# Three products of a weight conversion change engines: two from GpSimd to VectorE, one from VectorE to GpSimd

## The chip, the cores and the metric

The kernel runs on one core of one Trainium2 chip. A core has a matrix engine (TensorE, PE in the profile, with its weight loads shown as PEld), a vector engine (VectorE, DVE), a scalar engine (ScalarE, ACT), a general engine (GpSimd, POOL) and SyncE (SP), which here only starts transfers. Each engine runs its own list of instructions in order and waits for others through semaphores. The metric is the device time of one execution in microseconds, less is better; a time is the median of the runs shown. Before the change it is 257.74 us, the median of 3 runs from 257.5 to 257.95.

## The reference

A linear attention with product features is followed by a two-layer perceptron with exact GELU:

```python
def phi(x):                                   # r = 8, so 64 features
    a = np.einsum('rd,bhsd->bhsr', S1, x)
    b = np.einsum('rd,bhsd->bhsr', S2, x)
    return np.einsum('bhsi,bhsj->bhsij', a, b).reshape(*x.shape[:-1], r * r)
q_p, k_p = (phi(q), phi(k))                   # q, k, v: (4, 4, 1088, 32) float32
kv = np.einsum('bhsf,bhsd->bhfd', k_p, v)
z = np.sum(k_p, axis=2)
num = np.einsum('bhsf,bhfd->bhsd', q_p, kv)
den = np.einsum('bhsf,bhf->bhs', q_p, z)[..., None] + 1e-06
x = (num / den).transpose(0, 2, 1, 3).reshape(4352, 128)
h = x @ w_in                                  # w_in: (128, 2048) float64
g = 0.5 * h * (1.0 + erf(h / sqrt(2)))
out = g @ w_out                               # w_out: (2048, 128) float64
```

The two weights and the sketches S1 and S2 arrive as float64. The kernel computes in float32: it takes the two 32-bit words of each number apart and makes a float32 of them.

## The kernel before, in words

**Tiling.** The 4352 tokens are worked on as chunks of 512: two chunks for each of the four batches, and a ninth chunk that holds the 64 tokens left over of each batch. Tokens of a chunk lie in the free dimension, `xT[n]` being 128 x 512. For each chunk `hidden(n, fi)` multiplies one 128-column tile of w_in with `xT[n]` (line 770) and ScalarE applies GELU (line 777). There are 16 such tiles, fi = 0 to 15. The second product takes one of two forms. The first four tiles of chunk 0 and the first eight of chunk 1 are projected plainly (`project`, line 955). All others go through a Strassen-like scheme of seven products instead of eight, in blocks of four tiles: `token_sums` (lines 821 to 824, on GpSimd) makes four sums of a block's GELU outputs, `channel_sums` (lines 808 to 811, on GpSimd) makes four sums of each piece of w_out into the tiles T1 to T4, once, and `two_products` (line 856) multiplies them on TensorE, two products at a time, one in either half of the array's columns.

**Weights.** Both weights come in five pieces of 256, 256, 512, 512 and 512 columns: `w_in[0..4]` and `w_out[0..4]`. In the text, piece 4 of w_in is the last one, for the tiles fi = 12 to 15, and piece 2 of w_out the third one, for fi = 4 to 7. The class `Rounding` converts a piece. `fields` (VectorE, lines 283 and 288) cuts exponent and mantissa bits out of the high words; `low_words` and `exponents` (ScalarE, lines 270 and 294) scale the low words and rebias the exponents; `mantissas` (VectorE, line 302) joins the mantissa's two parts; `signs` (VectorE, line 307) adds the sign to the exponent; `product` (line 312) multiplies mantissa and signed power of two into the float32 weight. `product` takes the engine as an argument, VectorE unless told otherwise; `finish` is mantissas, signs and product on VectorE.

**Order.** The order of every engine's list is the order of the text; nothing is planned at run time. After a start in which the first attention chunk is made, a loop walks over steps t, one `hidden` call each. Steps 0 to 3 are tiles 0 to 3 of chunk 0, steps 4 to 11 tiles 0 to 7 of chunk 1, steps 12 to 23 the other tiles of chunk 0, steps 24 to 31 the other tiles of chunk 1, then chunk after chunk. Steps 0 to 3 have their side work written out by hand: there the pieces 0 and 1 of w_out are converted, with their products on GpSimd, and `ratio` (lines 686 to 700) makes chunk 1's `xT` on VectorE. At step 4 the projections of chunk 0's tiles 0 to 3 (two of them issued at step 3 already) and the two halves of chunk 1's first hidden product (`first_hidden`, line 786) follow. Later steps have lists `slots[t]`, filled by `at(t, f, ...)` in the order in which the calls are written. The six pieces from index 2 on are converted in turns, w_in before w_out: the fields of a turn are cut before the turn in front of it is ended. `end` of w_in's last piece stands in step 12, that of w_out's last piece in step 13, behind the two transposes of the next keys (`key_turn_blocks`, line 383). The channel sums of pieces 1, 0, 2, 3 and 4 stand in steps 5, 6, 13, 16 and 18. `widen_v_rem(1)` (line 366, GpSimd) in step 12 waits for a transfer. The token sums of chunk 0's blocks are issued at steps 15, 19 and 23, and their products start four, three and three steps later.

**What later work reads.** The projections of chunk 0 read w_out's pieces 0 and 1. `hidden` of steps 20 to 23 reads w_in's last piece. The seven-product blocks read T1 to T4 and the token sums.

Of the kernel before, what the change touches and what calls it, by code (L numbers as in the profile page):

```python
# [16 lines left out]
def kernel(  # L17
# [18 lines left out]
    pe, dve, act, pool, sp = nc.tensor, nc.vector, nc.scalar, nc.gpsimd, nc.sync  # L36
# [31 lines left out]
    def work_banks():  # L68

        return wps.tile([128, 2, CW], FP, name="w_ps")  # L70
# [505 lines left out]
    def expand_copy(n, i):  # L576
        A[i] = att.tile([128, 2, CW // 2], FP, name="A_sb")
        act.copy(out=A[i][:, :, :width[n] // 2], in_=B_of[n, i][:, :, :width[n] // 2])

    def expand_multiply(n, i):  # L580
        W = width[n]
        a, b = (t.rearrange("f g (r x) -> f g r x", r=2) for t in (A[i][:, :, :W // 2], B_of[n, i][:, :, W // 2:W]))
        dve.tensor_mul(out=qp[n].rearrange("f r (g x) -> f g r x", g=G)[:, 2 * i:2 * i + 2], in0=a, in1=b)  # L583
# [90 lines left out]
    def ratio_products(n, banks):  # L674

        for s in range(2):
            for c in range(NP):
                rows = slice(c * F, (c + 1) * F)
                for r in range(2):
                    for i, (h, w) in enumerate(((2 * c + r, kz_apart[rows, r, c, :D]), (2 * (1 - c) + r, z_cols[rows, r]))):  # L680
                        pe.matmul(banks[h * D:(h + 1) * D, i, s * HW:(s + 1) * HW], lhsT=w,
                                  rhs=qp[n][rows, r, s * HW:(s + 1) * HW], start=True, stop=True)

    def ratio_turn(banks):
        turned = att.tile([128, 2 * CW], FP, name="q_f", bufs=1)
        dve.transpose(out=turned[:, :CW], in_=banks[:, 1])
        return turned

    def ratio(n, banks, turned):

        den = att.tile([128, NP, 2 * H], FP, name="den_tok").rearrange("p c k -> p (c k)")
        first = turned[:, :CW].rearrange("p (k x) -> p k x", x=D)[:, :, 0]
        for c in range(NP):
            dve.tensor_scalar(out=den[c * F:(c + 1) * F], in0=first[(1 - c) * F:(2 - c) * F], scalar1=1e-6, scalar2=None, op0=AX.add)
        dve.reciprocal(out=den, in_=den)
        xT[n] = att.tile([128, CW], FP, name="xT", bufs=3)
        for s in range(2):
            wide = turned[:, CW + s * HW:CW + (s + 1) * HW]
            dve.transpose(out=wide, in_=den[:, s * 8:(s + 1) * 8, None].broadcast_to([128, 8, D]))
            dve.tensor_mul(out=xT[n][:, s * HW:(s + 1) * HW], in0=banks[:, 0, s * HW:(s + 1) * HW], in1=wide)  # L700
# [63 lines left out]
    def hidden(n, fi, by_halves=False):  # L764
        W = width[n]
        ps = first_banks.pop((n, fi)) if (n, fi) in first_banks else hidden_bank()
        w = w_tile(w_in_sb, fi)
        for rows in (slice(0, 64), slice(64, 128)) if by_halves else (slice(0, 128),):
            if (n, fi) not in begun:
                pe.matmul(ps[rows, :W], lhsT=w[:, rows], rhs=xT[n][:, :W], start=True, stop=True)  # L770
        if n < NCH and fi < USUAL[n]:
            g_of[n, fi] = mlp.tile([128, CW], FP, name="g", bufs=4)
        else:
            if fi % NB == 0:
                blocks[n, fi // NB] = block(FP)
            g_of[n, fi] = blocks[n, fi // NB][:, fi % NB]
        act.activation(out=g_of[n, fi][:, :W], in_=ps[:, :W], func=ACT.Gelu)  # L777

    def first_hidden(n, half):

        if half == 0:
            first_banks[n, 0] = hidden_bank()
        parts = 1 if n else 2
        for i in range(parts):
            cols = slice(half * 256 + i * 256 // parts, half * 256 + (i + 1) * 256 // parts)
            pe.matmul(first_banks[n, 0][:, cols], lhsT=w_tile(w_in_sb, 0), rhs=xT[n][:, cols], start=True, stop=True)  # L786
# [53 lines left out]
    def first_block(n):  # L840
        return USUAL[n] // NB if n < NCH else 0
# [102 lines left out]
    def project(n, fi, parts=range(B // 2), cols=slice(None)):  # L944
        first, final = fi == (BLOCKED if n == NMAIN else 0), fi == (USUAL[n] if n < NCH else NF) - 1
        if first and n not in o_of:
            o_of[n] = out_bank() if n < NMAIN else [out_bank() for i in range(B // 2)]
        g = g_of[n, fi]
        if n == NMAIN:

            for i in parts:
                pe.matmul(o_of[n][i][:, :128], lhsT=g[:, i * 128:(i + 1) * 128], rhs=w_tile(w_out_sb, fi),  # L952
                          start=first, stop=final)
            return
        pe.matmul(o_of[n][:, cols], lhsT=w_tile(w_out_sb, fi), rhs=g[:, cols], start=first, stop=final)  # L955
# [35 lines left out]
    r = Rounding(SR)  # L991
# [43 lines left out]
    w_out = [Rounding(w, beside=b) for w, b in zip(w_out_sb[:2], w_in)]  # L1035
# [28 lines left out]
    def at(t, f, *a):  # L1064
        slots[t].append(lambda: f(*a))
# [88 lines left out]
    rounding = {}  # L1154

    def begin(w):

        rounding[w.name] = Rounding(w)
        rounding[w.name].fields()

    def by_scalar(w, *what):
        for f in what:
            getattr(rounding[w.name], f)()

    def end(w):
        rounding[w.name].finish()

    turns = [w[i] for i in range(2, 5) for w in (w_in_sb, w_out_sb)]
    both, low, exp = ("low_words", "exponents"), ("low_words",), ("exponents",)
    schedule = (((4, exp),), ((5, low), (6, exp)), ((7, both),), ((8, low), (9, exp)), ((10, both),), ((11, low), (12, exp)))  # L1170
    for k, acts in enumerate(schedule):
        t1 = acts[-1][0]
        if k + 1 < len(turns):
            at(t1, begin, turns[k + 1])
        for t, what in acts:
            at(t, by_scalar, turns[k], *what)
        if k + 1 < len(turns):
            at(t1, end, turns[k])
    at(12, widen_v_rem, 1)
    for i, t in ((1, 5), (0, 6), (2, 13)):  # L1180
        at(t, channel_sums, i)
    at(16, channel_sums, 3)
    for r in range(2):
        at(13, key_turn_blocks, 1, r)
    at(13, end, turns[-1])
    at(16, features_of_all, 1)
    at(16, outer_of_all, 1)
# [93 lines left out]
    for t in range(len(steps) + LAG):  # L1281
        if t < 4:

            hidden(0, t)
            if t == 0:
                expand_multiply(1, 0)
                w_out[0].fields()
                expand_copy(1, 1)
                expand_multiply(1, 1)
            if t == 1:  # L1290
                w_out[0].low_words()
                w_out[0].exponents()
                w_out[0].mantissas()
                w_out[0].signs()
                w_out[0].product(pool)
                w_out[1].fields()
            if t == 2:
                w_out[1].low_words()
            if t == 3:
                banks = work_banks()  # L1300
                ratio_products(1, banks)
                w_out[1].mantissas()
                w_out[1].exponents()
                turned = ratio_turn(banks)
                w_out[1].signs()
                w_out[1].product(pool)
                ratio(1, banks, turned)
                project(0, 0)
                project(0, 1)
            continue  # L1310
        if t == 4:
            begin(turns[0])
            by_scalar(turns[0], *low)
            for f, *a in products[t] + products[t + 1]:
                f(*a)
            for half in range(2):
                first_hidden(1, half)
        for n in drains[t]:
            drain(n)
        sooner = t == NMAIN * NF  # L1320
        if sooner:
            for f, *a in products[t]:
                f(*a)
        if t < len(steps):
            n, fi = steps[t]
            hidden(n, fi, by_halves=t >= 18)
        if t < len(steps) and steps[t][0] < NMAIN and steps[t][1] % NB == NB - 1:
            n, b = steps[t][0], steps[t][1] // NB
            if b >= first_block(n):
                token_sums(n, b)  # L1330
        for f in slots[t]:
            f()
        for n in done[t]:
            store(n)
        if t not in (4, 5) and not sooner:
            for f, *a in products[t]:
                f(*a)
# [41 lines left out]
```

## Time and profile before

| what | value |
|---|---|
| median of 3 runs | 257.74 us (257.5 to 257.95) |
| the profiled execution's own time | 257.98 us |
| its span in the profile | 256.1 us |
| PE busy | 252.0 us, 98% |
| DVE busy | 160.8 us, 63% |
| ACT busy | 113.4 us, 44% |
| POOL busy | 177.4 us, 69% |
| granted TensorE clock | 0.999 |

Starts in the profile are counted from the beginning of the span; 1.88 us of the execution's own time lie around it. A row of the timeline has the start, the duration, the engine, the line, the operation, the tile written and the tiles read, the shape and the count; what stands in brackets at its end is the idle time of the engine just before it and what ended that. A float32 matrix product appears as two weight loads and two matmuls, so a 512-column product of one tile is two rows. Instructions of one engine overlap a little: a VectorE row of 0.42 us is followed by the next after 0.34 us where nothing ties them, and a 128x512 GpSimd row of 1.28 us after 1.23 us.

### The profile page before, as it was taken

The page shows a single profiled execution, that of the slowest core. Times are in us where ns is not written, and L with a number is a line of the kernel's source. Part 1 is how long each engine was busy: PE and PEld are TensorE (multiplying, and loading weights), DVE is VectorE, ACT ScalarE, POOL GpSimd, SP SyncE. Part 2 cuts the span into 40 slices and gives each one's busy share as a digit, 9 for nine tenths or more (in the row PEclk, how much of TensorE's full clock was granted, in tenths as well). Part 3 has the DMA queues.
Part 4 walks back from the last instruction along what each step waited for, and adds up shares of the span by engine and source line. Part 5 has one row for each costly group of instructions (what it writes and reads, how often), then busy time and mean ns, then how long its engine had stood idle before and what let it go on. Part 6 is the DMA issues. An engine that isn't in the chain of part 4 may idle for free.

```text
span 256.1 us, 5989 instructions
## 1 busy us (share of the span) xinstructions
PE 252.0 (98%) x2421; PEld 131.9 (52%) x2421; DVE 160.8 (63%) x333; ACT 113.4 (44%) x219; POOL 177.4 (69%) x194
## 2 busy tenths in 40 slices
PE   8999999999999999999999999999999999999995
PEld 4844443555454545454444455455544444445784
DVE  3899999979798987580278976399307000700382
ACT  3683885323535333533335332623444334433541
POOL 3527438997849787587758774787758777877950
PEclk9999999999999999999999999999999999999999
DMA  6699648710001101102000002000200200020021
GB/s 205 185 282 315 185 113 217 191 18 8 0 3 16 25 4 26 18 13 31 3 0 0 0 15 32 1 4 0 39 5 7 38 0 3 5 36 3 0 36 31
DMA packets 29083, 13.50 MB, mean 53 GB/s; under 512 B 21888, under 2 KB 27264, under 8 KB 29056
## 3 DMA queue, kind: packets, MB, share of 16 engines
q1 hardware_dynamic: 28624, 12.79, 20.6%
q8 instruction: 19, 0.31, 0.5%
q10 hardware_dynamic: 432, 0.33, 0.4%
q14 instruction: 8, 0.07, 0.1%
HBM read 10.88 MB, written 2.23 MB: 51 GB/s over the span
## 4 chain that ended last, share of the span: by engine, by line
PE 97%; DVE 1%; POOL 0%; issue 0%; ACT 0%
PE h_ps L770 44%; PE o_ps L856 35%; PE o_ps L955 4%; PE w_ps L926 2%; PE w_ps L456 1%; PE w_ps L606 1%; PE w_ps L661 1%; PE w_ps L987 1%; PE w_ps L572 1%; PE o_ps L952 1%; PE h_ps L348 1%; PE o_ps L445 1%; PE w_ps L1074 1%; DVE q_pT L583 0%; POOL w_out L312 0%; PE h_ps L786 0%
## 5 line engine op out<-in xcount | busy, mean ns | idle before, releaser
L770 PE MATMUL h_ps<-xT,w_in 128*64 128x512 f32 (+2 forms) x536 | 137.1, 567 | 0.0
L777 ACT ACTIVATE block<-h_ps 128x512 f32<-128x512 f32 (+1 forms) x132 | 75.4, 571 | 119.1 <-PE h_ps L770 117.2
L856 PE MATMUL o_ps<-block,w_out 128*64 128x256 f32 x232 | 59.5, 379 | 0.0
L821 POOL TENSOR_TENSOR bits_low<-block 128x512 f32<-128x512 f32 x29 | 37.4, 1291 | 30.8 <-ACT block L777 30.8
L770 PEld LDWEIGHTS h_ps<-xT,w_in 128*64 128x64 f32 (+1 forms) x536 | 40.9, 140 | 27.0 <-issue 8.5
L856 PEld LDWEIGHTS o_ps<-block,w_out 128*64 128x64 f32 x232 | 31.7, 137 | 39.2 <-issue 28.2
L822 POOL TENSOR_TENSOR bits_a<-block 128x512 f32<-128x512 f32 x29 | 37.3, 1285 | 12.6 <-ACT block L777 12.6
L871 DVE COPY sums<-o_ps 64x256 f32<-64x256 f32 x8 | 3.3, 417 | 60.2 <-PE o_ps L856 60.2
L823 POOL TENSOR_TENSOR bits_e<-bits_a,block 128x512 f32<-128x512 f32 x29 | 37.6, 1298 | 2.3
L824 POOL TENSOR_TENSOR bits_m<-block,bits_e 128x512 f32<-128x512 f32 x29 | 37.6, 1298 | 2.3
L856 PE MATMUL o_ps<-block,small 128*64 128x256 f32 x116 | 29.8, 379 | 0.0
L856 PE MATMUL o_ps<-bits_low,small 128*64 128x256 f32 x116 | 29.8, 379 | 0.0
L856 PE MATMUL o_ps<-bits_a,small 128*64 128x256 f32 x116 | 29.8, 379 | 0.0
L856 PE MATMUL o_ps<-bits_m,w_out 128*64 128x256 f32 x116 | 29.8, 379 | 0.0
L856 PEld LDWEIGHTS o_ps<-block,small 128*64 128x64 f32 x116 | 15.7, 137 | 18.6 <-issue 11.1
L856 PE MATMUL o_ps<-bits_e,small 128*64 128x256 f32 x116 | 17.7, 383 | 0.0
L856 PEld LDWEIGHTS o_ps<-bits_m,w_out 128*64 128x64 f32 x116 | 15.9, 137 | 0.0
L856 PEld LDWEIGHTS o_ps<-bits_a,small 128*64 128x64 f32 x116 | 15.8, 137 | 0.0
L856 PEld LDWEIGHTS o_ps<-bits_low,small 128*64 128x64 f32 x116 | 15.7, 137 | 0.0
L618 DVE STREAM_TRANSPOSE w_ps<-w_ps 128x512 f32<-128x512 f32 (+1 forms) x7 | 4.8, 688 | 17.1 <-ACT xT L672 12.7
L856 PEld LDWEIGHTS o_ps<-bits_e,small 128*64 128x64 f32 x116 | 7.9, 137 | 11.4 <-issue 9.5
L955 PE MATMUL o_ps<-g,w_out 128*128 128x512 f32 x24 | 12.1, 601 | 0.1
(222 smaller groups left out, 320.4 us busy)
## 6 DMA issues: line engine op xcount, KB each, us to landing
block<-in_moe_w_in_dram SPq DMA_DIRECT2D x3, 512.0 KB, 10.6
block<-in_moe_w_out_dram SPq DMA_DIRECT2D x3, 512.0 KB, 11.1
k<-in_k_dram SPq DMA_DIRECT2D x12, 128.0 KB, 2.8
v<-in_v_dram SPq DMA_DIRECT2D x12, 128.0 KB, 3.1
q<-in_q_dram SPq DMA_DIRECT2D x24, 64.0 KB, 2.8
out_dram<-oT SPq DMA_DIRECT2D x21, 64.0 KB, 2.2
q_first<-in_q_dram SPq DMA_DIRECT2D x2, 256.0 KB, 4.1
v<-in_v_dram SPq DMA_DIRECT2D x2, 256.0 KB, 4.7
```

The lines of the kernel that those rows point to most:

```text
L348: pe.transpose(ps[:, i * 128:(i + 1) * 128], in_=s, identity=ident)
L618: dve.transpose(out=tok, in_=ps[:, :, :H2])
L770: pe.matmul(ps[rows, :W], lhsT=w[:, rows], rhs=xT[n][:, :W], start=True, stop=True)
L777: act.activation(out=g_of[n, fi][:, :W], in_=ps[:, :W], func=ACT.Gelu)
L821: pool.tensor_sub(out=s[3], in0=a11, in1=a21)
L822: pool.tensor_add(out=s[1], in0=a21, in1=a22)
L823: pool.tensor_sub(out=s[2], in0=s[1], in1=a11)
L824: pool.tensor_sub(out=s[4], in0=a12, in1=s[2])
L856: pe.matmul(acc[n][bank][half * 64:(half + 1) * 64, col:col + HW], lhsT=fixed, rhs=moving, start=opens and e == 0 and name in "4715", stop ...
L871: dve.tensor_copy(out=N[lo, 0, one], in_=a0[lo, one])
L926: pe.matmul(acc[NMAIN][rows, COLS_REM[name]], lhsT=tokens[:, rows], rhs=fixed, start=k == 0 and name == ORDER_REM[0], stop=k == BLOCKED // ...
L955: pe.matmul(o_of[n][:, cols], lhsT=w_tile(w_out_sb, fi), rhs=g[:, cols], start=first, stop=final)
```

## The change

The products of w_out's pieces 0 and 1, in steps 1 and 3, go from GpSimd to VectorE, at the place in VectorE's list where they are written: behind the piece's `signs`, and for piece 1 ahead of `ratio`. The product of w_in's last piece leaves VectorE's list in step 12 and joins GpSimd's list in the same step, behind `widen_v_rem(1)` and ahead of the channel sums of w_out's third piece in step 13. Nothing else is moved, and the same operations are done on the same operands.

```diff
     def end(w):
-        rounding[w.name].finish()
+        r = rounding[w.name]
+        r.mantissas()
+        r.signs()
+        if w is not turns[4]:
+            r.product()
+
+    def multiply(w):
+        rounding[w.name].product(pool)
...
     at(12, widen_v_rem, 1)
+    at(12, multiply, turns[4])
     for i, t in ((1, 5), (0, 6), (2, 13)):
         at(t, channel_sums, i)
...
             if t == 1:
                 w_out[0].low_words()
                 w_out[0].exponents()
-                w_out[0].mantissas()
-                w_out[0].signs()
-                w_out[0].product(pool)
+                w_out[0].finish()
                 w_out[1].fields()
...
                 turned = ratio_turn(banks)
                 w_out[1].signs()
-                w_out[1].product(pool)
+                w_out[1].product()
                 ratio(1, banks, turned)
```

`turns[4]` is w_in's last piece.

## The prediction

> **What bounds the kernel now.** I read the page's first and fourth parts, then the waits of the weight loads, then the timelines of the two stretches that the change touches.
>
> ```profile
> span 256.1 us, 5989 instructions
> PE 252.0 (98%) x2421; PEld 131.9 (52%) x2421; DVE 160.8 (63%) x333; ACT 113.4 (44%) x219; POOL 177.4 (69%) x194
> ...
> PE 97%; DVE 1%; POOL 0%; issue 0%; ACT 0%
> ```
>
> TensorE is the chain. From 24.3 us to 240 us its busy time equals the stretch in the table of windows, so in there nothing can be won, but every wait that the change puts on TensorE is lost for good. Gains can only come from the start, and its waits of weight loads (14 to 26 us) name the products that the change moves:
>
> ```profile
> PEld o_ps L955 <- POOL w_out L312: 1.4, 2, 0.9
> ```
>
> In the timeline the place looks so:
>
> ```profile
> 19.04 0.79 DVE L302 SCALAR_TENSOR_TENSOR bits_m<-bits_a,bits_low 128x256 f32<-128x256 uint32 x1
> 19.75 0.70 DVE L686 STREAM_TRANSPOSE q_f<-w_ps 128x512 f32<-128x512 f32 x1
> 20.38 0.38 DVE L307 SCALAR_TENSOR_TENSOR bits_e<-small,bits_r 128x256 uint32<-128x256 uint32 x1
> 20.79 0.81 DVE L694 TENSOR_SCALAR den_tok<-q_f 64x16 f32<-64x16 f32 x2
> ...
> 23.21 0.42 DVE L700 TENSOR_TENSOR xT<-w_ps,q_f 128x256 f32<-128x256 f32 x1
> ...
> 18.61 0.94 POOL L312 TENSOR_TENSOR w_out<-bits_m,bits_e 128x256 f32<-128x256 f32 x1 [4.23 <-DVE bits_e L307]
> 20.84 0.73 POOL L312 TENSOR_TENSOR w_out<-bits_m,bits_e 128x256 f32<-128x256 f32 x1 [1.29 <-DVE bits_e L307]
> ...
> 21.62 0.30 PEld L955 LDWEIGHTS o_ps<-g,w_out 128*128 128x128 f32 x2 [0.87 <-POOL w_out L312]
> ```
>
> The reader should see two things. Each product's end releases a weight load. And VectorE's L302 takes 0.79 us beside the first product where its other 128x256 rows take 0.42, and L694's pair takes 0.81 (0.17 and 0.63) beside the second: the engines hold each other up.
>
> The second place is GpSimd's list from 35 us on:
>
> ```profile
> 35.15 0.45 POOL L366 COPY v_rem_aug<-v_rem 64x128 f32<-64x128 f32 x1 [6.96 <-DMA v_rem<-in_v_dram]
> ...
> 39.13 1.32 POOL L821 TENSOR_TENSOR bits_low<-block 128x512 f32<-128x512 f32 x1 [1.70 <-ACT block L777]
> 40.73 1.51 POOL L822 TENSOR_TENSOR bits_a<-block 128x512 f32<-128x512 f32 x1 [0.27 <-ACT block L777]
> ...
> 49.13 1.28 POOL L821 TENSOR_TENSOR bits_low<-block 128x512 f32<-128x512 f32 x1
> ...
> 50.48 0.14 PEld L856 LDWEIGHTS o_ps<-block,small 128*64 128x64 f32 x1 [0.29 <-POOL bits_low L821]
> ```
>
> From 40.73 to 59.6 us GpSimd never idles, and the sum that starts at 49.13 ends at 50.41, just 0.07 us ahead of the weight load that needs it. That load's matmul starts at 50.91. In the start's row a load follows GpSimd's end by 0.05 us and the matmul follows the load by 0.10, so the sum may end as late as 50.74 to 50.76: a slack of about 0.34 us, against a GpSimd list that the change makes longer.
>
> **The start, part by part.** *Removed:* two GpSimd products, 0.94 and 0.73 us. What TensorE loses by them: the last product ahead of the first projection (line 681) leaves the array at about 19.30 (four groups 0.215 us apart, the last at 19.09), and the first matmul starts at 19.70, so 0.40 us. Four matmuls at 0.43 us end at 21.42, and the fifth starts at 21.72: 0.30 us. At most 0.70 us are to be had.
>
> *Added to VectorE:* the same two products at 0.42 us each, from the row of w_in's piece 1 (L312 at 15.83). The first follows the signs (18.11 + 0.42) at 18.57, ends at 18.99, and pushes what is behind it by 0.34 us plus the wait for the signs, 0.46 together. `bits_m` of piece 1 then starts at 19.45, alone, takes 0.42 instead of 0.79, and the transpose L686 starts at 19.80, as against 19.75. Signs at 20.43 to 20.81, second product 20.85 to 21.27, as against 21.57 on GpSimd. L694 starts at 21.30 instead of 20.79. Its pair takes 0.37 us undisturbed, 0.81 if the channel sums that now start at 21.35 disturb it as the product did; so its end is 21.67 to 21.86 if about half of that comes, before 21.60. The rest of `ratio` is a chain of 2.0 us, so chunk 1's second half is ready at 23.70 to 23.89, before 23.63.
>
> *What is late next on TensorE:* first projections 19.31 to 21.03, the next four matmuls from 21.42 (21.27 + 0.15) to 23.15, first half of L786 to 23.58, and then the second half must wait for xT: 23.85 to 24.04 instead of 23.88. So of the 0.70 us nothing arrives: the sum of the start is -0.03 to +0.16 us, and I take +0.05. If nothing disturbs L694 and its wait for the product's end vanishes, xT comes at 23.5 and the end is -0.25. No transfer is issued by these instructions and neither queue changes; ScalarE's exponents of piece 1 (19.19) start some 0.05 us later, hidden by their 0.6 us to the signs.
>
> **w_in's last product.** *Removed from VectorE:* 0.69 us at 38.63 (0.61 to the next start). No wait of TensorE hangs on it: the tiles that read it come in step 20, at about 46 us.
>
> *Added to GpSimd:* one 128x512 product. None is shown; the 128x256 ones undisturbed take 0.73 to 0.75, the 128x512 sums 1.28 against 0.45 for the 128x128 ones, so I take 1.28, or 1.23 to the next start. Bounds: 0.94 (disturbed, half size) and 1.61 (the longest 128x512 row).
>
> *The wait it adds:* GpSimd now stands still until VectorE has the signs of that piece. VectorE's fields in front of it (L288 at 35.37, 1.76 us) were held up by the channel sums that now stand behind the product; undisturbed by them they end at 36.0, then mantissas from 35.95 and signs from 36.55 to 37.24. So the product runs from 37.3 to 38.55; if VectorE brings 0.2 us of lateness from the start, from 37.5. Queued behind it: the third piece's channel sums (1.80 us; before 35.56 to 37.4, in what was idle time), the token sums of chunk 0's first block (5.19 undisturbed), two more channel sums (3.55), and the sum that TensorE waits for in step 22 (1.28). Of VectorE's list the mantissas, signs and product of w_out's last piece fall into that, each with two operands in SBUF: in the profile they lengthened the three sums beside them by 0.23, 0.32 and 0.33 us, and I keep 0.9 for them.
>
> Sum: 37.3 + 1.23 + 1.80 + 5.19 + 0.9 + 3.55 + 1.28 = 51.25, before 50.41. The two idle times of 1.70 and 0.27 us have taken up only part of the wait and the product. With the other bounds (start 37.5, product 1.61, or no disturbance at all, 0.94) it is 50.1 to 51.85. The matmul can start 0.16 us behind: 51.4 to 51.5 instead of 50.91, a wait of about 0.55 us, between 0 and 1.1. Because that wait ends on GpSimd's clock, the start's +0.05 (or -0.25) vanishes in it. The token sums behind have their own slack (the next is needed 0.5 us or more after its end), and TensorE has no idle time later that could give it back.
>
> So 0.6 us with a small lateness from VectorE: against the profiled execution 257.98 + 0.6 = 258.6, and that execution stands 0.24 us above the median of the runs, so 258.35 us.
>
> **Rivals.** *Slower still, VectorE starved.* The field cutting at 35.37 waited through three GpSimd sums until a gap between two that depend on each other. The three operations of w_out's last piece now need three such gaps: inside the channel sums, between the second and third token sum, and between the third and fourth, so that the product ends at about 45.4 instead of 44.48. This 0.9 us is covered: VectorE waits 0.51 us for TensorE at 54.84, and TensorE itself is late by 0.55. If one operation misses its gap, the next is in the channel sums at about 47.8; then the key sums (L1104, end 53.13) come 3.9 us later, past the 1.3 us by which they lead L456 at 54.45, and TensorE loses some 2.6 us: 260.3 us. Against it stands that each operation is issued over 1 us ahead of its gap. The Trainium skill (SBUF — State Buffer, section Who interferes with whom) describes an exclusive lock that is held for the whole of one instruction; by it VectorE would come in after a single GpSimd instruction, the product would end near 41 us, and this rival would be out, with the forecast unchanged. The row of 1.76 us, beside three sums, speaks against so short a wait, and I keep the rival.
>
> *Faster: no wait in step 22.* If the three VectorE operations cost GpSimd nothing, the sum ends at 50.35, and TensorE keeps what the start gives: -0.25 us to +0.16, so 257.6. It decides at a delay of GpSimd below 0.3 us. To pass 0.2% (0.5 us, about what a measurement of this kernel can tell from no change), xT would also have to be ready at 23.2, that is, VectorE would need to win back more than the two products cost; all of the 0.70 us gives 257.05. For this speaks only that VectorE loses 0.37 and 0.45 us to GpSimd there now.
>
> *No change of weight:* GpSimd's delay is 0.3 to 0.6 us, 258.0; this is the forecast's lower half.
>
> **How the numbers follow.** The forecast (a wait in step 22, +0.25 to +0.95) gets 0.62, and 0.38 of that lies above 0.5 us, 0.24 below. No wait there gets 0.21, of which 0.11 is faster by over 0.2%, more than its arithmetic gives, because VectorE's order among the locks is only bounded. Starved or later than the bounds: 0.17. So faster 0.11, same 0.34, slower 0.55. The forecast's own range is 258.0 to 258.7; with the rivals 257.4 to 259.0, which leaves out about 0.08 below and 0.1 above.
>
> **What would show it.** Right: L312 of w_out on VectorE at 18.6 and 20.9; L955 without a wait for POOL at the first projection; L786's second half waiting for xT; L302 and L694 shorter or displaced as above; L312 of w_in on POOL at 37.3; L821 of the second block ending near 51.3, and L856 at 51.4 with TensorE idle before it. Wrong: that L821 ending before 50.7, or TensorE's step 4 reaching line 770 at 24.0 or before.

## The result, and the profile after

The changed kernel takes 258.72 us (median of 9 runs, 258.22 to 259.59), the kernel before 257.74 us (9 runs, 257.23 to 258.12). The ratio is 1.0042, with a 95% interval of 1.0027 to 1.0058: slower by 0.98 us, where 0.6 us had been forecast. That stands just above the forecast's own range (+0.25 to +0.95 us, or 258.0 to 258.7) and inside the wider one with the rivals (257.4 to 259.0). The profiled execution is one of the slower ones of the changed kernel, 259.27 us, with a span of 257.5 us.

The page of the changed kernel, its first and fourth part and one group of the fifth (busy time, mean, and behind the second bar the idle time ahead of the group and what ended it):

```profile
span 257.5 us, 5987 instructions
PE 252.0 (98%) x2421; PEld 131.2 (51%) x2421; DVE 159.5 (62%) x334; ACT 113.6 (44%) x219; POOL 176.8 (69%) x193
...
PE 81%; DMA 6%; POOL 6%; SPq 4%; ACT 1%; issue 1%; DVE 0%; POOLq 0%
...
L856 PE MATMUL o_ps<-bits_low,small 128*64 128x256 f32 x116 | 29.9, 380 | 1.3 <-POOL bits_low L821 1.3
```

The same group on the page of before:

```profile
L856 PE MATMUL o_ps<-bits_low,small 128*64 128x256 f32 x116 | 29.8, 379 | 0.0
```

TensorE does the same 252.0 us of work, but the chain is no longer TensorE's alone: 16% of it run over GpSimd, the transfers and their queue, and a wait of 1.3 us for a GpSimd sum has come in where the page of before has none.

The start, on VectorE's timeline:

```profile
17.08 0.42 DVE L302 SCALAR_TENSOR_TENSOR bits_m<-bits_a,bits_low 128x256 f32<-128x256 uint32 x1
...
17.86 0.43 DVE L312 TENSOR_TENSOR w_out<-bits_m,bits_e 128x256 f32<-128x256 f32 x1
...
18.83 0.43 DVE L302 SCALAR_TENSOR_TENSOR bits_m<-bits_a,bits_low 128x256 f32<-128x256 uint32 x1
...
20.22 0.42 DVE L312 TENSOR_TENSOR w_out<-bits_m,bits_e 128x256 f32<-128x256 f32 x1
20.68 0.40 DVE L694 TENSOR_SCALAR den_tok<-q_f 64x16 f32<-64x16 f32 x2
...
22.68 0.42 DVE L700 TENSOR_TENSOR xT<-w_ps,q_f 128x256 f32<-128x256 f32 x1
```

The second L302 takes 0.43 us instead of 0.79 and the L694 pair 0.40 instead of 0.81: without a GpSimd product beside them nothing holds them up. This whole stretch begins 0.69 us earlier than in the profile of before, at 17.08 instead of 17.77, ahead of anything that was changed. That differs from one execution to the next (17.08 to 17.78 in ten profiles, whichever the kernel), so from here on the profiles are compared by times counted from this first `bits_m`. The first row of each pair below is that `bits_m`, the second the first line 770 behind step 4; the first pair is the kernel before, the second the changed one:

```profile
17.77 0.42 DVE L302 SCALAR_TENSOR_TENSOR bits_m<-bits_a,bits_low 128x256 f32<-128x256 uint32 x1
24.31 1.98 PE L770 MATMUL h_ps<-xT,w_in 128*128 128x512 f32 x4
...
17.08 0.42 DVE L302 SCALAR_TENSOR_TENSOR bits_m<-bits_a,bits_low 128x256 f32<-128x256 uint32 x1
23.70 1.98 PE L770 MATMUL h_ps<-xT,w_in 128*128 128x512 f32 x4
```

So counted, line 770 comes at 6.54 us before and at 6.62 after.

The second place, on GpSimd's timeline and then on TensorE's:

```profile
37.65 0.75 POOL L366 COPY v_rem_aug<-v_rem 64x128 f32<-64x128 f32 x1 [10.46 <-DMA v_rem<-in_v_dram]
38.36 1.29 POOL L312 TENSOR_TENSOR w_in<-bits_m,bits_e 128x512 f32<-128x512 f32 x1
...
40.97 0.79 POOL L811 TENSOR_TENSOR small<-w_out,small 128x128 f32<-128x128 f32 x1
41.72 1.72 POOL L821 TENSOR_TENSOR bits_low<-block 128x512 f32<-128x512 f32 x1
...
50.91 1.27 POOL L821 TENSOR_TENSOR bits_low<-block 128x512 f32<-128x512 f32 x1
```

```profile
50.30 0.59 PE L856 MATMUL o_ps<-block,small 128*64 128x256 f32 x2
52.23 0.43 PE L856 MATMUL o_ps<-bits_low,small 128*64 128x256 f32 x1 [1.33 <-POOL bits_low L821]
```

The sum for step 22 ends at 52.18 us and releases the matmul at 52.23. Its partner in the other half of the array was ready and started at 50.30; its two matmuls ran for 0.59 us, which is why TensorE's idle time is only 1.33 us. Before, the same matmul started without a wait:

```profile
50.92 0.38 PE L856 MATMUL o_ps<-bits_low,small 128*64 128x256 f32 x1
```

The matmul that waits comes at 35.15 us from the first `bits_m`, and at 33.15 before: 2.00 us later, and the end of the span comes 2.09 us later, 240.42 instead of 238.33. The 0.08 us of the start vanish in the 2.00, because GpSimd's sum ends the wait. The 0.09 us left over come behind that matmul, and they are no more than the rounding of the two spans to 0.1 us.

VectorE's list shows why nothing else suffers:

```profile
35.77 0.68 DVE L307 SCALAR_TENSOR_TENSOR bits_e<-block,bits_r 128x512 uint32<-128x512 uint32 x1
...
38.17 3.27 DVE L307 SCALAR_TENSOR_TENSOR bits_e<-block,bits_r 128x512 uint32<-128x512 uint32 x1
41.47 0.83 DVE L312 TENSOR_TENSOR w_out<-bits_m,bits_e 128x512 f32<-128x512 f32 x1
...
56.21 0.23 DVE L511 TENSOR_TENSOR z_s<-w_ps,sT 128x64 f32<-128x64 f32 x1 [4.05 <-PE w_ps L456]
```

The signs that GpSimd's product needs end at 36.45; GpSimd does not use them before 38.36, because its list still stands at the copy that waits for a transfer. The signs of w_out's last piece are held up for 3.27 us, yet VectorE is early and waits 4.05 us for TensorE later on.

### The profile page after: what moved, and what is told of

Same layout as the page of the kernel before. It is cut to its first block, busy times and chain, and to the rows that moved or that the text cites. A ratio compares the mean times of both kernels' runs of the same rounds, so it can differ in the third digit from the quotient of the medians.

```text
span 257.5 us, 5987 instructions
## 1 busy us (share of the span) xinstructions
PE 252.0 (98%) x2421; PEld 131.2 (51%) x2421; DVE 159.5 (62%) x334; ACT 113.6 (44%) x219; POOL 176.8 (69%) x193
## 4 chain that ended last, share of the span: by engine, by line
PE 81%; DMA 6%; POOL 6%; SPq 4%; ACT 1%; issue 1%; DVE 0%; POOLq 0%
PE h_ps L770 38%; PE o_ps L856 33%; DMA block<-in_moe_w_out_dram 6%; PE w_ps L926 2%; SPq L125 2%; PE w_ps L456 1%; PE w_ps L606 1%; PE w_ps L661 1%; PE w_ps L987 1%; POOL bits_low L821 1%; DMA v_rem<-in_v_dram 1%; SPq L181 1%; PE o_ps L952 1%; POOL small L811 1%; POOL bits_m L824 0%
## 5 line engine op out<-in xcount | busy, mean ns | idle before, releaser
L821 POOL TENSOR_TENSOR bits_low<-block 128x512 f32<-128x512 f32 x29 | 38.0, 1311 | 28.9 <-ACT block L777 28.9
L823 POOL TENSOR_TENSOR bits_e<-bits_a,block 128x512 f32<-128x512 f32 x29 | 37.3, 1288 | 2.3
L824 POOL TENSOR_TENSOR bits_m<-block,bits_e 128x512 f32<-128x512 f32 x29 | 37.0, 1277 | 2.3
L856 PEld LDWEIGHTS o_ps<-block,small 128*64 128x64 f32 x116 | 15.6, 137 | 18.5 <-issue 11.1
## 6 DMA issues: line engine op xcount, KB each, us to landing
block<-in_moe_w_out_dram SPq DMA_DIRECT2D x3, 512.0 KB, 12.8
```

The source lines that it names most:

```text
L821: pool.tensor_sub(out=s[3], in0=a11, in1=a21)
L823: pool.tensor_sub(out=s[2], in0=s[1], in1=a11)
L824: pool.tensor_sub(out=s[4], in0=a12, in1=s[2])
L856: pe.matmul(acc[n][bank][half * 64:(half + 1) * 64, col:col + HW], lhsT=fixed, rhs=moving, start=opens and e == 0 and name in "4715", stop ...
```

## The experiments

Two theories stood against each other. G: the loss arises on GpSimd's list, which gets the product and its waits, and shows in step 22. S: it arises at the start, where VectorE gets two products. Within G it was open how much of it is work, and how much the transfer for which the copy of line 366 waits. An edit is shown against the changed kernel, unless the text names the kernel before; three dots stand for lines left out. The first four kernels are compared with 31 runs of the kernel before (median 257.72 us), the other four with 33 (median 257.80 us).

**The first half alone.**

```diff
     def end(w):
         r = rounding[w.name]
         r.mantissas()
         r.signs()
-        if w is not turns[4]:
-            r.product()
+        r.product()
...
-    at(12, multiply, turns[4])
```

> Only the first half of the change: both w_out products on VectorE, w_in's last product stays on VectorE. Theory G (the loss arises on GpSimd's list: the copy of the remaining values, which waits for a transfer, then the product and the channel sums, so that the second block's first token sum ends too late for step 22): no loss, 257.6 to 257.9 us, and no wait for L821 in step 22. Rival S (the loss arises at the start, because the two products delay chunk 1's xT): the whole loss is here, 258.6 to 258.8 us, with TensorE reaching line 770 of step 5 about 1 us later than before, measured from the same product of step 0.

257.83 us against 257.72 of before, ratio 1.0006 (0.9993 to 1.0019). In its timeline GpSimd's sum is on time, and both weight loads of step 22 come together:

```profile
48.60 1.28 POOL L821 TENSOR_TENSOR bits_low<-block 128x512 f32<-128x512 f32 x1
```

```profile
49.90 0.14 PEld L856 LDWEIGHTS o_ps<-block,small 128*64 128x64 f32 x1 [0.29 <-POOL bits_low L821]
49.93 0.13 PEld L856 LDWEIGHTS o_ps<-bits_low,small 128*64 128x64 f32 x1
```

Line 770 comes 6.61 us behind the first `bits_m`, against 6.54, and the span ends 0.06 us later, so counted. S is out: the whole loss that it expected here is missing.

**The second half alone.** Both w_out products stay on GpSimd:

```diff
-                w_out[0].finish()
+                w_out[0].mantissas()
+                w_out[0].signs()
+                w_out[0].product(pool)
...
-                w_out[1].product()
+                w_out[1].product(pool)
```

> Only the second half: w_in's last product on GpSimd behind the copy of the remaining values, both w_out products still on GpSimd. Theory G: the whole loss, 258.4 to 259.2 us, the more of it the later the transfer of the remaining values lands (35.1 us before, 37.5 after), with TensorE idle ahead of L856 in step 22. Rival S: 257.7 us, as before.

258.52 us, ratio 1.0035 (1.0022 to 1.0048): nearly the whole loss. Here the transfer landed in time (34.3 us), and the product waited for VectorE, as the forecast had it:

```profile
34.31 0.37 POOL L366 COPY v_rem_aug<-v_rem 64x128 f32<-64x128 f32 x1 [6.69 <-DMA v_rem<-in_v_dram]
36.59 1.30 POOL L312 TENSOR_TENSOR w_in<-bits_m,bits_e 128x512 f32<-128x512 f32 x1 [1.90 <-DVE bits_e L307]
37.84 0.91 POOL L808 TENSOR_TENSOR small<-w_out 128x128 f32<-128x128 f32 x1
38.71 0.90 POOL L809 TENSOR_TENSOR small<-w_out 128x128 f32<-128x128 f32 x1
39.57 0.90 POOL L810 TENSOR_TENSOR small<-w_out,small 128x128 f32<-128x128 f32 x1
...
49.71 1.28 POOL L821 TENSOR_TENSOR bits_low<-block 128x512 f32<-128x512 f32 x1
```

Three channel sums take 0.90 us where they take 0.45 alone: each lets one of VectorE's three operations through. The sum ends at 50.99, 14.48 us behind VectorE's signs at 36.51, and TensorE loses 0.71 us in step 22.

**The product ahead of the copy that waits.**

```diff
-    at(12, widen_v_rem, 1)
     at(12, multiply, turns[4])
+    at(12, widen_v_rem, 1)
```

> The whole change, but the product stands ahead of the copy that waits for the transfer. The product then runs in the time of that wait, from about 36.6 to 37.9 us. If the transfer's wait ahead of the product is most of the loss (G with the transfer): 257.8 to 258.2 us. If it is only the amount of work that GpSimd gets (G without the transfer, my forecast's sum, where the product waited for VectorE's signs): 258.3 to 258.6 us. Rival S: 258.7 us.

258.47 us, ratio 1.0032 (1.0021 to 1.0044), scattering only from 258.09 to 258.89 in 9 runs. The expectation for the amount of work held, the one for the transfer as most of the loss did not: with the signs at 36.40 the sum ends at 51.01, 14.61 us later.

**The product behind the channel sums.**

```diff
     at(12, widen_v_rem, 1)
-    at(12, multiply, turns[4])
...
+    at(13, multiply, turns[4])
     at(16, channel_sums, 3)
```

> The whole change, but the product stands behind the third piece's channel sums. If VectorE's signs held the product up, as my forecast had it, the sums now run while GpSimd would wait, and the loss falls to 0 to 0.3 us: 257.7 to 258.1. If the transfer holds up the whole list (G with the transfer), the order of the two behind it is of no account and the time stays at 258.4 to 259.0 us when the transfer lands late, as in the profile of after, and falls only when it lands at 35 us.

258.40 us, ratio 1.0028 (1.0014 to 1.0042), scattering most of these first four, from 257.68 to 259.78. In the profiled execution the transfer held the list up until 36.5 us, so the sums had no idle time to run in, and the sum of step 22 ended 14.37 us behind the signs. This agrees with the transfer as the gate of GpSimd's list, but the order alone wins little in such an execution, and no profile shows one in which the transfer was early.

**The copy moved out of the way.**

```diff
-    at(12, widen_v_rem, 1)
     at(12, multiply, turns[4])
...
     at(18, channel_sums, 4)
+    at(20, widen_v_rem, 1)
```

> The whole change, but the copy of the remaining values, with its wait for the transfer, stands in step 20, behind the second block's token sums. If what counts is GpSimd's work between VectorE's signs (36.5 us) and the sum of step 22, the 0.73 us of fill and copy that the version with the product first had in that stretch fall away: the sum ends near 50.3 us, TensorE waits 0.1 to 0.2 us, and the time is 257.8 to 258.1 us. If the loss has another place, 258.4 us as before. Either way the runs should scatter less than those of the whole change, since no late transfer can hold the list up.

258.57 us, ratio 1.0030 (1.0019 to 1.0040), from 258.02 to 258.87. My 257.8 to 258.1 was wrong: the fill and copy (0.73 us) are gone, but the channel sums again ran against VectorE at 0.90 us each, and the sum ended 14.49 us behind the signs, as in the second half alone. What the transfer adds to the median is the difference to the whole change, 0.15 us between the two times and 0.21 between their losses; the two intervals overlap, so it is not told apart from nothing. In the late execution shown above the sum ended 15.73 - 14.49 = 1.24 us later behind the signs than here, the smaller cost of VectorE's operations there included. The scatter shrank as expected, from 1.37 us in 9 runs to 0.85 in 10.

**The slack, by itself.** The kernel before, with the fourth piece's channel sums made a second time:

```diff
     at(16, channel_sums, 3)
+    at(16, channel_sums, 3)
```

> The kernel before, with the four channel sums of the fourth piece made twice in step 16 (the same values again): 1.77 us more on GpSimd's list, nothing else. It measures the slack of GpSimd's list against step 22. With a slack of about 0.3 us the time rises by 1.4 to 1.5 us, to 259.1 to 259.2 us. If GpSimd's list had more slack than that, or the loss of the change came from VectorE, it rises by less than 0.7 us.

258.87 us against 257.80, ratio 1.0056 (1.0035 to 1.0078); the medians differ by 1.07 us, and the ratio is lifted by one run of 262.12. The median stays 0.2 to 0.3 us below the 259.1 to 259.2 that were expected, and the place is as expected: 1.77 us of work on GpSimd, with nothing else changed, bring the same wait in the same place:

```profile
L856 PE MATMUL o_ps<-bits_low,small 128*64 128x256 f32 x116 | 29.9, 380 | 0.7 <-POOL bits_low L821 0.7
```

Counted from the first `bits_m`, the matmul of step 22 comes 1.31 us later and the span ends 1.36 us later, so the slack is 0.41 to 0.46 us by the profiles, and 1.77 - 1.07 = 0.70 us by the medians; the forecast had read 0.34 from the profile of before.

**The copy later, in the kernel before.**

```diff
-    at(12, widen_v_rem, 1)
...
     at(18, channel_sums, 4)
+    at(20, widen_v_rem, 1)
```

> The kernel before, with only the copy of the remaining values moved to step 20. Before, GpSimd idles 1.7 us behind the channel sums of the third piece, so nothing can be won: 257.5 to 257.9 us. If the transfer's landing costs the kernel before time in many executions, the time falls by more than 0.3 us.

257.65 us, ratio 0.9998 (0.9989 to 1.0006): as expected, nothing. The channel sums then run at 29.7 us, and the first token sum still waits for ScalarE, now 6.22 us.

**The change with its work placed in GpSimd's idle time.**

```diff
-    for i, t in ((1, 5), (0, 6), (2, 13)):
+    for i, t in ((1, 5), (0, 6), (2, 8)):
...
-    at(12, widen_v_rem, 1)
     at(12, multiply, turns[4])
...
     at(18, channel_sums, 4)
+    at(20, widen_v_rem, 1)
```

> The whole change, with the copy of the remaining values in step 20 and the third piece's channel sums in step 8, where GpSimd waits for nothing to do. Both products stay where the change put them, w_in's last one with its wait for VectorE's signs. GpSimd's list then is behind the product at 37.8 us, ahead of the first token sum's GELU output (39 us), so that the loss is gone altogether: 257.6 to 257.9 us. If the product on GpSimd itself (its wait, or the lock with VectorE) cost time, 258.2 us or more stay.

257.75 us, ratio 0.9997 (0.9984 to 1.0010). The product is where the change put it, with its wait and with VectorE beside it, and the loss is gone:

```profile
37.62 1.30 POOL L312 TENSOR_TENSOR w_in<-bits_m,bits_e 128x512 f32<-128x512 f32 x1 [5.10 <-DVE bits_e L307]
38.88 1.71 POOL L821 TENSOR_TENSOR bits_low<-block 128x512 f32<-128x512 f32 x1
...
48.83 1.28 POOL L821 TENSOR_TENSOR bits_low<-block 128x512 f32<-128x512 f32 x1
```

With the copy moved alone, 0.77 us of loss were left (258.57 us); moving the channel sums took them away. So neither the engine nor the wait costs time as such. What costs is that the product, the channel sums and the token sums stand in one list between VectorE's signs and step 22.

One table holds the profiles together, each line's times counted from its first `bits_m`, in us:

| kernel | line 770 behind step 4 | waiting matmul of step 22 | end of span | difference of the last two |
|---|---|---|---|---|
| before | 6.54 | 33.15 | 238.33 | 205.18 |
| first half alone | 6.61 | 33.22 | 238.39 | 205.17 |
| second half alone | 6.55 | 33.86 | 239.11 | 205.25 |
| product ahead of the copy | 6.62 | 33.93 | 239.17 | 205.24 |
| product behind the sums | 6.62 | 33.69 | 238.97 | 205.28 |
| copy later | 6.60 | 33.83 | 239.12 | 205.29 |
| before, sums twice | 6.53 | 34.46 | 239.69 | 205.23 |
| before, copy later | 6.53 | 33.14 | 238.33 | 205.19 |
| sums early, copy later | 6.61 | 33.22 | 238.37 | 205.15 |
| the whole change | 6.62 | 35.15 | 240.42 | 205.27 |

The ends of the spans, and with them the last column, are good to 0.05 us. That column moves by 0.14 us at most: whatever the kernel loses, it has lost by the time of that matmul, and it gets nothing back.

## Why the prediction was right, and where its sizes were off

**The direction and the place.** Slower, by a wait for L821 in step 22 that runs through to the end. The place is shown by the wait itself, by the last column of the table, and by two kernels that move it at will: GpSimd's list lengthened without the change brings it, and the list relieved with the change in place takes it away.

**The start.** "-0.03 to +0.16 us, and I take +0.05" came out as +0.06 to +0.08 in the profiles. The steps behind it hold too: L302 took 0.43 us where 0.42 was stated, L694's pair 0.40, close to its undisturbed 0.37, the first projection came earlier (1.66 us behind the first `bits_m` instead of 1.83), and the second half of L786 waited for xT. One of the forecast's signs of being wrong, line 770 at 24.0 us or before, is there to the letter, at 23.70, and only because this execution's start is 0.69 us early; counted from `bits_m` it is not. The statement that this would vanish in the later wait holds for the kernels in which GpSimd sets the end of that wait.

**The second half's sum.** The forecast put the sum of step 22 14.01 us behind the end of VectorE's signs (51.25 - 37.24). In the profile of the changed kernel it came 15.73 us behind them. Counted from the first `bits_m`, the forecast's bounds for its end (50.1 to 51.85) are 32.33 to 34.08 us, and it ended at 35.10: this execution belongs to the rival "later than the bounds", while the median lies 0.37 us above the forecast's 258.35. Two terms were too small:

- The step "the product runs from 37.3" took VectorE's signs as the last thing that GpSimd waits for. In the changed kernel's profile the transfer of line 366 was: it let the copy start at 37.65, the copy took 0.75 us, and the product began 1.91 us behind the signs instead of 0.06. I had quoted that wait of 6.96 us and its end at 35.15 us, and treated the end as fixed. It is not: the copy starts at 34.25 to 37.65 us in the profiles in which it stands in step 12 ahead of all other work of that step. In the median it is a small term, 0.15 to 0.21 us by the kernel without it, and not told apart from nothing.
- "I keep 0.9" for the three VectorE operations was 1.35 us, three times 0.45, in the second half alone and with the copy later, and 0.44 + 0.34 in the whole change's profile, where the copy took some of it (0.75 us instead of 0.45). I had taken it from sums that were hit in part.

Without a late transfer the delay of the matmul is 0.71 us (33.86 - 33.15 in the table, the second half alone; 0.80 us between the medians), where the forecast had about 0.5: its 51.25 + 0.16 against 50.91. The longer sums add 0.47 (14.48 - 14.01); against it stand signs that came 0.15 us earlier than forecast, 19.32 us behind the first `bits_m` instead of 19.47, and a matmul that follows the sum after 0.06 us instead of 0.16.

**The rivals.** VectorE starved did not happen, though an operation was blocked for 3.27 us: w_out's last product ended at 42.30 us, because VectorE had come to that stretch over 2 us earlier than before, without w_in's product and without the channel sums beside its field cutting. The forecast had counted that relief only for the signs. *No wait in step 22* is what the kernel with the sums early shows, at 257.75 us; there the start's 0.07 us stay, below what the times can tell.

**How VectorE and GpSimd take turns.** In the second half alone one VectorE operation gets in per channel sum, and each such sum takes 0.90 us instead of 0.45. In the whole change it is otherwise: L307's row starts at 38.17, GpSimd began and ended its product and three channel sums, and only around 40.97, where L811 waits for L810, did L307 come in. What decides between the two patterns was not tried and stays open. The Trainium skill (SBUF — State Buffer, section Who interferes with whom) describes a lock held for the whole of one instruction, whose loser blocks. The second half alone agrees with it in form; what the prediction worked out from it and doubted, that VectorE would come in after a single GpSimd instruction, is refuted by the row of 3.27 us.

## What to carry to other kernels

Where one engine is busy without a gap, look for the others' last arrivals ahead of it and measure their slack by adding work to their list: here 1.77 us added and 1.07 to 1.36 us lost gave the 0.4 to 0.7 us that this change had to stay below. A product that is moved to an engine with 30% idle time still lengthens that engine's list at one spot, so the question is what stands behind it there; the same product cost nothing once the channel sums behind it ran in step 8 and the copy in step 20. And a wait for a transfer in a list gates everything behind it at a time that differed by 3.4 us between profiles. Work that needs no transfer is safer ahead of it, though here the median gained only 0.15 to 0.25 us by that, which is not told apart from nothing.

## What the runs showed of the hardware that I had not expected

The same transfer released the same copy at 34.25, 34.31, 35.15, 35.15, 36.49 and 37.65 us in six profiles, each of another kernel. The lateness is there when the transfer is issued: SyncE's rows for `v_rem` start at 32.83 us before and at 35.23 after, and the copy starts 2.2 to 2.8 us behind them in all six. It does not come with the change: in the kernel with the product ahead of the copy and in the one with the sums early, which hold both halves of it, these rows start at 31.29 and 31.05. Between the profiles of before and after the weights' transfers in front of it took a median of 10.6 and 11.1 us against 13.0 and 12.8 from issue to landing; what sets this was not tried. The start of VectorE's first `bits_m` differs by up to 0.70 us between executions, where the runs of the kernel before differ by 1.01 us in all (257.18 to 258.19 in the comparison with the first half alone); it has to be taken out before profiles of single executions are compared.
